# A pooled-attention and two-expert-stage kernel: the shared row tile's scores from one unpadded q, in a newly searched order

## The chip, the cores and the metric

The kernel runs on one core of one Trainium2 chip, as one program of 8,648 instructions in the profiled execution. The metric is the device time of one execution in microseconds, the median of several. TensorE (PE) multiplies matrices, VectorE (DVE), ScalarE (ACT) and GpSimd (POOL) work element by element, and SyncE (SP) issues all DMAs in order of one list.

## The reference, cut to what matters

Three stages follow each other. The change lies in the first.

```python
# 1. attention over keys and values that are averaged in groups of 8: B = 8, H = 8, S = 576, D = 64, Sp = 72
k_p = k.reshape(B, H, Sp, 8, D).mean(axis=3);  v_p = v.reshape(B, H, Sp, 8, D).mean(axis=3)
scores = np.matmul(q, k_p.transpose(0, 1, 3, 2)) / np.sqrt(D)
scores = scores - np.max(scores, axis=-1, keepdims=True)
attn = np.exp(scores); attn = attn / (np.sum(attn, axis=-1, keepdims=True) + 1e-09)
x = np.matmul(attn, v_p)                       # -> 4608 rows of 512
# 2. soft mixture of experts: 32 slots, softmax over rows into slots, w1, relu, w2, softmax over slots back
logits = x @ phi
# 3. x @ w_in (512 x 1024), h * softmax(h), layer norm, @ w_out (1024 x 512)
```

Inputs are float32: q, k and v 9.4 MB each, w1 and w2 16.8 MB each, w_in and w_out 2.1 MB each (handed over as 64-bit words that the kernel turns into float32, so 4.2 MB each are read). The output is 9.4 MB.

## The kernel before, in words

**Tiling.** The 4608 rows are 36 row tiles of 128 tokens. Three row tiles are a block (n = 0 to 11), and three blocks hold the 1152 tokens of two neighbouring batches b = 2p and 2p + 1. A batch has 576 tokens, that is four and a half row tiles, so the middle tile of the middle block (n = 1, 4, 7, 10; r = 1) holds 64 tokens of each of two batches: the shared row tile. Heads are taken in four pairs hp. `key_sums` and `key_matrix` lay the 72 pooled keys of both heads of a pair out as a matrix BD of 128 x 144 with zeros between the heads.

**The scores.** `scores(n, hp)` makes one 128 x 144 result in PSUM for each of the three row tiles: the stationary operand is q (64 + 64 rows of two heads, 128 tokens), the moving one BD. For the shared tile the kernel before keeps q in two copies of 128 columns, the first with zeros where the second batch's tokens are and the other the other way round. `load_q` loads its halves in two DMAs (L144, L145), `query_zero` writes the zeros (L371, on POOL), and two full products add up in PSUM (L386). In the trace every float32 matmul has two records, so a pair of heads of a plain block has 6 and one of blocks 1, 4, 7, 10 has 8.

**After the scores**, DVE takes row maxima (M, L394) and differences (A, L398), ACT exponentials (E), DVE their sums (U), POOL and DVE the inverse (R, r), POOL the products with it (N, L435). PE turns the result (T, L441), ACT copies it out, PE multiplies by what the values and phi give (P, X, w, x) to logits (L, L457), and weighted sums of the rows go into pG (G, L544). POOL sums the values (V), PE lays them out by key (Y, L337).

**What sets the order.** All engines run in a hand-kept order: a string of step names (`order = ...`), in which the letters above are followed by the block or batch and the piece. Each engine takes its instructions in the order of that string. The loads of q, k, v and of eight weight pieces are steps too (`ik4`, `iq7`, `ia2.0`, `ib0.0`, `io0`), so the string also is SP's order. Loads go into a ring of 88 KB in each partition in a fixed sequence of tiles, and a load waits until the tiles that it writes over have been read. SP waits with it, and all loads behind. Every load also uses one of eight DMA semaphores in turn, so it waits for the load eight places ahead to have landed. D0 to D6 are loads into the buffers of the attention stage when these come free.

**Behind the attention** stands a second string (`steps = ...`): the products with w1 (A) and w2 (B0 to B15, one for each half of an expert, L1005), the conversion of w_out and w_in (a, b, s, t, + ; `o`, `i`, `j`), the turned combine weights (p0 to p8, `combine_turn`, L976), column sums of w_out (c0 to c7, `out_sums`, L1011 and L1012). The third stage then runs over the 36 row tiles.

Of the kernel before, what the change touches and what calls it, by code (L numbers as in the profile page):

```python
# [19 lines left out]
P = 128  # L20
NP = 4
NB = 3
NR = 3
# [62 lines left out]
def moe_attention_kernel(ctx: ExitStack, tc, q, k, v, phi, w1, w2, w_in, w_out, g, out):  # L86
# [48 lines left out]
    def q_tile(n):  # L135

        nr = NR + (n % NB == 1)
        qT[n] = ring.tile([P, HP, nr, P], F32, name=f"qT{n}")

    def load_q(n, h0=0, h1=HP):  # L140
        if n % NB == 1:
            dst = qT[n].rearrange("p h r t -> p h (r t)")[:, h0:h1]
            src = q[n].rearrange("p (h x) -> p h x", h=HP)[:, h0:h1]
            sp.dma_start(dst[:, :, 0:192], src[:, :, 0:192])  # L144
            sp.dma_start(dst[:, :, 320:512], src[:, :, 192:384])  # L145
        else:
            sp.dma_start(qT[n][:, h0:h1], q[n].rearrange("p (h r t) -> p h r t", h=HP, r=NR)[:, h0:h1])
# [108 lines left out]
    if True:  # L256
# [113 lines left out]
        def query_zero(n):  # L370
            pool.memset(qT[n].rearrange("p h r t -> p h (r t)")[:, :, 192:320], 0.0)  # L371

# [7 lines left out]
        def scores(n, hp):  # L380
            sc = st["sc", n, hp] = psA.tile([P, NR, 2, J], F32, tag="sc", bufs=PT["sc"][1], name=f"sc{n}{hp}")
            x = 0
            for r in range(NR):
                hv = halves(n, r)
                for i, (b, _, _) in enumerate(hv):
                    pe.matmul(sc[:, r].rearrange("p h j -> p (h j)"), qT[n][:, hp, x, :], BD[b % NBD][:, hp, :],  # L386
                              start=(i == 0), stop=(i == len(hv) - 1))
                    x += 1
# [354 lines left out]
        for n in range(NBLK):  # L743
            if n % NB == 1:
                step(f"B{n}", query_zero, n)
# [44 lines left out]
        for x, f in zip("D0 D1 D2 D3 D4 D5 D6".split(), (scores_done, sums_done, third_group, third_slots, logits_done, fourth_group,  # L790
# [4 lines left out]
        order = ("K0.0 K0.1 k0.0 k0.1 S0.0 S0.1 K0.2 K0.3 M0.0 M0.1 A0.0 k0.3 k0.2 E0.0 E0.1 S0.2 S0.3 F0 F1 F2 F3 F4 F5 F6 F7 M0.2 U0.0 A0.2 M0.3 "  # L795
# [26 lines left out]
                 "D1 D5 e0 e1 e2 la2 lt0 es lt1 lT0 lT1 ld0 ld1 lT2 ls0 ls1 lz lo0 cs lo1 ge4").split()  # L822
        assert sorted(order) == sorted(steps)
        for x in order:
            f, args = steps[x]
            f(*args)

# [684 lines left out]
```

## Time and profile before

| what | value |
|---|---|
| three runs | 410.56, 411.17, 414.97 us; median 411.17 |
| the profiled execution | 410.22 us, span 408.4 us, mean granted clock 0.992 |
| busy share of the span | PE 94%, DVE 76%, ACT 71%, POOL 54% |
| moved by DMA | 97.09 MB; read from HBM 70.32 MB, written 9.44 MB |
| chain that ended last, by engine | PE 70%, DMA 11%, DVE 8%, POOL 4%, ACT 3% |

The span is the time from the first to the last instruction, and 1.8 us lie around it. The page cuts the span into 40 slices of 10.2 us. The attention stage is slices 1 to 12, the weights keep arriving until slice 18, and from slice 20 on the third stage repeats itself. PE's busy share is the sum of its records and is near full nearly everywhere, so the chain of waits and the stretch-by-stretch table tell more than it does. Loads are counted in MB as the trace does: a k or v of one batch is 1.18 MB, a q of one block 0.79, a piece of w1 0.52 or 1.05, one of w2 or a raw piece 1.05.

### The profile page before, as it was taken

The numbers are of one execution on the slowest core, as the hardware profiler recorded it, in microseconds if no ns is written. First come the engines' busy times: TensorE is split into PE (matmuls) and PEld (weight loads), VectorE is DVE, ScalarE is ACT, GpSimd is POOL, SyncE is SP. The second block draws the span as 40 slices with busy tenths as digits, with TensorE's granted clock in tenths as the row PEclk, the third lists the DMA queues.
The fourth block names the chain that finished last, engine by engine and source line by source line (L and its number), as shares of the span: only waits on it lengthen the run. The fifth ranks groups of instructions, "written<-read, shape, count | busy, mean of one in ns | idle before, by whom it ended". The sixth has DMA issues, their size and how long they took to land.

```text
span 408.4 us, 8648 instructions
## 1 busy us (share of the span) xinstructions
PE 383.1 (94%) x3242; PEld 231.5 (57%) x3242; DVE 310.7 (76%) x492; ACT 288.2 (71%) x600; POOL 219.9 (54%) x408
## 2 busy tenths in 40 slices
PE   3889999999999698798999999999999999999996
PEld 2868988999987153333455444444444444444445
DVE  3899979999746757965899867877777777877720
ACT  2589988988876457935699847777666776667721
POOL 4289997879630120000345776776676666766620
PEclk9999999999999899899999999999999999999999
DMA  8999999899999999990001767776667566575761
GB/s 266 391 401 377 379 315 378 314 418 413 404 373 386 416 420 411 412 412 37 0 1 28 176 121 173 175 156 128 165 95 170 147 123 165 93 172 144 124 180 51
DMA packets 86217, 97.09 MB, mean 238 GB/s; under 512 B 69920, under 2 KB 74784, under 8 KB 80416
## 3 DMA queue, kind: packets, MB, share of 16 engines
q1 hardware_dynamic: 86176, 96.55, 73.9%
q8 instruction: 25, 0.41, 0.4%
q14 instruction: 16, 0.13, 0.1%
HBM read 70.32 MB, written 9.44 MB: 195 GB/s over the span
## 4 chain that ended last, share of the span: by engine, by line
PE 70%; DMA 11%; DVE 8%; POOL 4%; ACT 3%; issue 2%; SPq 1%; DVEq 0%; POOLq 0%
PE o L1344 14%; PE o L1342 13%; PE o L1341 13%; PE sc L386 7%; PE pt L441 5%; PE plt L457 4%; DMA raw<-in_w_in_dram 3%; PE h L1251 3%; DMA w<-in_w_dram 3%; PE pG L544 3%; DMA early<-in_w_dram 2%; DMA kT<-in_k_dram 1%; POOL a_rows L435 1%; DVE early L312 1%; PE pc L976 1%
## 5 line engine op out<-in xcount | busy, mean ns | idle before, releaser
L1341 PE MATMUL o<-W_hi,vhi 128*128 128x512 f16 x280 | 106.2, 379 | 0.1
L1342 PE MATMUL o<-W_lo,vhi 128*128 128x512 f16 x280 | 106.2, 379 | 0.0
L1344 PE MATMUL o<-W_hi,vlo 128*128 128x512 f16 x280 | 66.9, 380 | 0.2 <-DMA vlo<-v 0.2
L1263 ACT ACTIVATE e<-h,nm 128x1024 f32<-128x1024 f32 x33 | 36.7, 1113 | 40.8 <-DVE nm L1256 40.8
L386 PE MATMUL sc<-early,qT 128*128 128x144 f32 x320 | 49.2, 304 | 8.1 <-ACT early L318 7.7
L1322 DVE TENSOR_TENSOR v<-v,v 128x1024 f16<-128x1024 f32 x32 | 39.2, 1225 | 14.9 <-ACT v L1305 14.9
L386 PEld LDWEIGHTS sc<-early,qT 128*128 128x128 f32 x320 | 43.8, 201 | 10.3 <-POOL sel L289 5.0
L1341 PEld LDWEIGHTS <-vhi 128*128 128x128 f16 x280 | 27.4, 98 | 33.7 <-issue 1.1
L1342 PEld LDWEIGHTS <-vhi 128*128 128x128 f16 x280 | 27.4, 98 | 32.3 <-issue 0.4
L1256 DVE TENSOR_REDUCE nm<-h 128x1 f32<-128x1024 f32 x33 | 40.4, 1223 | 5.8 <-PE h L1251 5.7
L1344 PEld LDWEIGHTS <-vlo 128*128 128x128 f16 x280 | 25.1, 98 | 33.7 <-issue 7.4
L1269 DVE CUSTOM_DVE_ANT_0 u<-h,e 128x1024 f32<-128x1024 f32 x33 | 40.3, 1223 | 5.2 <-ACT e L1263 5.1
L1305 ACT ACTIVATE v<-u,b,sr 128x1024 f32<-128x1024 f32 x33 | 40.8, 1235 | 3.5 <-POOL b L1293 3.5
L435 POOL TENSOR_TENSOR a_rows<-a_rows,rs 128x864 f32<-128x864 f32 x24 | 39.2, 1633 | 6.4 <-DVE ssum L421 2.6
L1280 ACT ACTIVATE e<-u,nmu 128x1024 f32<-128x1024 f32 x33 | 37.9, 1148 | 0.5 <-POOL nmu L1275 0.3
L1318 DVE TENSOR_SCALAR v<-u,nmu,sr 128x1024 f16<-128x1024 f32 x32 | 26.0, 812 | 11.1 <-POOL sr L1291 11.1
L447 ACT ACTIVATE late<-pt 128x384 f32<-128x384 f32 x60 | 27.7, 488 | 5.8 <-PE pt L441 4.1
L1287 POOL TENSOR_TENSOR y<-y 128x1 f32<-128x1 f32 x33 | 30.2, 915 | 2.7
L1291 POOL TENSOR_TENSOR sr<-z,exponents 128x3 f32<-128x3 f32 x33 | 29.3, 887 | 2.7
L1275 POOL TENSOR_SCALAR nmu<-st 128x1 f32<-128x1 f32 x33 | 8.5, 258 | 40.2 <-DVE st L1269 40.2
L394 DVE TENSOR_REDUCE nmax<-sc 128x6 f32<-128x432 f32 x48 | 27.5, 590 | 3.0 <-PE sc L386 2.8
L441 PE MATMUL pt<-ident,a_rows 128*128 128x128 f32 x180 | 27.6, 280 | 1.5 <-POOL a_rows L435 1.1
(253 smaller groups left out, 741.4 us busy)
## 6 DMA issues: line engine op xcount, KB each, us to landing
w<-in_w_dram SPq DMA_DIRECT2D x16, 1024.0 KB, 11.8
vT<-in_v_dram SPq DMA_DIRECT2D x8, 1152.0 KB, 11.3
out_dram<-ob SPq DMA_DIRECT2D x11, 768.0 KB, 3.6
kT<-in_k_dram SPq DMA_DIRECT2D x7, 1152.0 KB, 9.7
w<-in_w_dram SPq DMA_DIRECT2D x12, 512.0 KB, 9.6
qT<-in_q_dram SPq DMA_DIRECT2D x7, 768.0 KB, 12.4
a_rows<-in_w_dram SPq DMA_DIRECT2D x4, 1024.0 KB, 8.6
qT<-in_q_dram SPq DMA_DIRECT2D x8, 384.0 KB, 11.5
```

The source lines that it names most:

```text
L386: pe.matmul(sc[:, r].rearrange("p h j -> p (h j)"), qT[n][:, hp, x, :], BD[b % NBD][:, hp, :], start=(i == 0), stop=(i == len(hv) - 1))
L435: eng.tensor_tensor(av, av, st["rs", n, hf].unsqueeze(3).to_broadcast([P, NR, 4, J]), ALU.mult)
L441: pe.transpose(pt[:, r, :], a_buf[n % NA][:, r, CH[c]:CH[c] + P], ident)
L1256: dve.tensor_reduce(nm, ft[i][0], axis=AX.X, op=ALU.max, negate=True)
L1263: act.activation(e, hv, AF.Exp, bias=nm, accum_out=st[:, 0:1])
L1269: dve.tensor_tensor_reduce(u, hv, e, 1.0, 0.0, ALU.mult, ALU.add, st[:, 1:2])
L1280: act.activation(e, u, AF.Square, bias=nmu, accum_out=st[:, 2:3])
L1305: act.activation(v, u, AF.Identity, bias=b, scale=sr[:, 0:1])
L1322: dve.tensor_tensor(v2, u_t[i]["v"], u_t[i]["v1"], ALU.subtract)
L1341: pe.matmul(po, hi[:, c, :], W_hi[:, c, :], start=(c == 0), stop=False)
L1342: pe.matmul(po, hi[:, c, :], W_lo[:, c, :], start=False, stop=False)
L1344: pe.matmul(po, lo[:, c, :], W_hi[:, c, :], start=False, stop=(c == NFC - 1))
```

## The change

`q_tile` and `load_q` make and load every block's q alike: three row tiles without padding, 6 KB in a partition in place of 8 for blocks 1, 4, 7, 10, in one DMA. `query_zero` and its four steps B1, B4, B7, B10 are gone. For the shared row tile `scores` issues two products of 64 stationary columns, each against its own batch's BD, into partitions 0 to 63 and 64 to 127 of the same result, with `tile_position` at column 0 and 64. The number of matmuls is the same. The string `order` is another one over its whole length (the same steps without the B's), and with it the order of all five engines up to the end of the attention stage, DMAs included; because the tiles are smaller, all loads lie at other places in the ring. In the second string three things stand elsewhere: c2 ahead of B12, c4 and c5 ahead of B13, and p8 behind B13 in place of behind B14, c6 and c7.

```diff
     def q_tile(n):
-
-        nr = NR + (n % NB == 1)
-        qT[n] = ring.tile([P, HP, nr, P], F32, name=f"qT{n}")
+        qT[n] = ring.tile([P, HP, NR, P], F32, name=f"qT{n}")
 
     def load_q(n, h0=0, h1=HP):
-        if n % NB == 1:
-            dst = qT[n].rearrange("p h r t -> p h (r t)")[:, h0:h1]
-            src = q[n].rearrange("p (h x) -> p h x", h=HP)[:, h0:h1]
-            sp.dma_start(dst[:, :, 0:192], src[:, :, 0:192])
-            sp.dma_start(dst[:, :, 320:512], src[:, :, 192:384])
-        else:
-            sp.dma_start(qT[n][:, h0:h1], q[n].rearrange("p (h r t) -> p h r t", h=HP, r=NR)[:, h0:h1])
+        sp.dma_start(qT[n][:, h0:h1], q[n].rearrange("p (h r t) -> p h r t", h=HP, r=NR)[:, h0:h1])
...
-        def query_zero(n):
-            pool.memset(qT[n].rearrange("p h r t -> p h (r t)")[:, :, 192:320], 0.0)
...
-            x = 0
             for r in range(NR):
-                hv = halves(n, r)
-                for i, (b, _, _) in enumerate(hv):
-                    pe.matmul(sc[:, r].rearrange("p h j -> p (h j)"), qT[n][:, hp, x, :], BD[b % NBD][:, hp, :],
-                              start=(i == 0), stop=(i == len(hv) - 1))
-                    x += 1
+                for b, t0, t1 in halves(n, r):
+                    pe.matmul(sc[t0:t1, r].rearrange("p h j -> p (h j)"), qT[n][:, hp, r, t0:t1], BD[b % NBD][:, hp, :],
+                              start=True, stop=True, tile_position=(0, t0))
...
-            if n % NB == 1:
-                step(f"B{n}", query_zero, n)
...
```

How the engines' orders read at three places follows; names are those of the built program, a row is an instruction with its output, its inputs and the output's shape.

PE, the last two pairs of heads of block 4 (pv is a turned set of values, sc the scores' result, qT q's tile, early holds BD, pt and a_rows belong to a turned result of an earlier block). Before:

```order
L337 MATMUL pv_585<-ident,early 72x128 x4
L441 MATMUL pt_590<-ident,a_rows_160 128x128 x3
L441 MATMUL pt_594<-ident,a_rows_160 128x128 x3
L386 MATMUL sc_598<-early,qT_114 128x144 x4
L386 MATMUL sc_603<-early,qT_114 128x144 x4
```

And of the change:

```order
L329 MATMUL pv_579<-ident,early 72x128 x4
L427 MATMUL pt_584<-ident,a_rows_159 128x128 x3
L427 MATMUL pt_588<-ident,a_rows_159 128x128 x3
L373 MATMUL sc_592<-early,qT_113 128x144
L373 MATMUL sc_592<-early,qT_113 64x144 x2
L373 MATMUL sc_592<-early,qT_113 128x144
L373 MATMUL sc_597<-early,qT_113 128x144
L373 MATMUL sc_597<-early,qT_113 64x144 x2
L373 MATMUL sc_597<-early,qT_113 128x144
```

Two of the four full products of each pair have become two of 64 rows; both stand between the same neighbours, pt ahead of them.

PE, the end of the products with w2, where the last pieces of w2 are waited for (p is their result, w_70 and w_74 the halves of the last expert, pcs the column sums, of which one row of each run is shown, pc the last turned weights, p8). Before:

```order
L1005 MATMUL p_2210<-w_64_2241,hTm 32x512 x4
...
L1011 MATMUL pcs<-W_hi,ones_h 128x512
...
L1005 MATMUL p_2210<-w_70_2243,hTm 32x512 x4
...
L1011 MATMUL pcs<-W_hi,ones_h 128x512
...
L976 MATMUL pc<-ident,L_all 32x128 x16
L1005 MATMUL p_2210<-w_74_2245,hTm 32x512 x4
```

And of the change:

```order
L989 MATMUL p_2202<-w_64_2233,hTm 32x512 x4
L960 MATMUL pc<-ident,L_all 32x128 x16
L989 MATMUL p_2202<-w_70_2235,hTm 32x512 x4
...
L995 MATMUL pcs<-W_hi,ones_h 128x512
...
L989 MATMUL p_2202<-w_74_2237,hTm 32x512 x4
```

pc has moved from behind w_70's products, right ahead of w_74's, to ahead of w_70's; the two column sums ahead of w_70 went further forward.

SP, the weight loads up to the first one of w2_00, which waits for the ring (w1_60 is a piece of w1 for expert 6, raw a piece of w_out). Before:

```order
L190 DMA w1_60_142<-in_w1_dram 128x1024
L190 DMA w1_10_133<-in_w1_dram 128x1024
L190 DMA w1_20_137<-in_w1_dram 128x1024
L190 DMA w1_62_143<-in_w1_dram 128x1024
L212 DMA raw_2042<-in_w_out_dram 128x2048
L190 DMA w2_00_146<-in_w2_dram 128x2048
```

And of the change:

```order
L182 DMA w1_62_142<-in_w1_dram 128x1024
L182 DMA w2_10_147<-in_w2_dram 128x2048
L182 DMA w1_12_133<-in_w1_dram 128x1024
L182 DMA w1_10_132<-in_w1_dram 128x1024
L182 DMA w2_00_145<-in_w2_dram 128x2048
```

The load of w2_00 waits in both for the value sums V6.2 (POOL L331 before, L323 now), before also for the scores S10.3. Ahead of it now stand two pieces of w1 fewer (w1_14 and w1_60 stand behind it), so that 36.7 MB of loads are ahead of it in SP's list and not 37.8.

## Rows read from the trace of the kernel before

**Rows 1.** the page's 40 slices: PE busy tenths, GB/s by DMA

```profile
...
PE   3889999999999698798999999999999999999996
...
GB/s 266 391 401 377 379 315 378 314 418 413 404 373 386 416 420 411 412 412 37 0 1 28 176 121 173 175 156 128 165 95 170 147 123 165 93 172 144 124 180 51
...
```

**Rows 2.** Stretches: length, busy PE PEld DVE ACT POOL, PEclk, DMA share, GB/s

```profile
...
16.00:36.00 20.00, 17.50 (x160) 15.62 (x162) 19.23 (x32) 15.92 (x55) 15.14 (x13) 1.00 1.03 399
36.00:60.00 24.00, 23.22 (x318) 20.56 (x314) 22.05 (x49) 22.78 (x81) 22.17 (x22) 1.00 0.95 344
60.00:80.00 20.00, 19.82 (x301) 18.07 (x292) 19.42 (x40) 16.92 (x56) 15.53 (x19) 1.00 0.94 344
80.00:108.00 28.00, 27.91 (x437) 26.09 (x428) 25.90 (x59) 23.77 (x60) 24.20 (x24) 1.00 1.02 415
108.00:128.00 20.00, 19.82 (x385) 16.59 (x384) 10.02 (x40) 14.12 (x39) 4.84 (x5) 1.00 0.99 372
128.00:184.00 56.00, 47.42 (x582) 21.22 (x585) 40.23 (x57) 34.18 (x54) 4.07 (x6) 0.94 1.01 414
...
```

**Rows 3.** DMA rows of the stretch 24 to 28 us

```profile
...
DMA packets 255, 1.67 MB, mean 419 GB/s; under 512 B 31, under 2 KB 31, under 8 KB 158
...
```

**Rows 4.** DMA rows of the stretch 28 to 32 us

```profile
...
DMA packets 1120, 1.42 MB, mean 356 GB/s; under 512 B 46, under 2 KB 1037, under 8 KB 1072
...
```

**Rows 5.** the chain of waits from 42 to 49 us: start us, us, what

```profile
...
42.02 0.44 PE pv L337 x4
...
43.15 1.96 PE sc L386 x16
...
46.58 0.25 PE pw L348 x11
46.83 1.67 PE sc L386 x12
...
```

**Rows 6.** the chain of waits from 84 to 93 us

```profile
...
85.96 1.86 PE pG L544 x56
...
```

**Rows 7.** POOL's instructions up to 130 us: busy us, mean ns, idle before

```profile
...
L371 POOL MEMSET qT<- 128x512 f32 x4 | 2.1, 520 | 0.1
...
```

**Rows 8.** the chain of waits of the whole program, by its longer pieces

```profile
...
124.80 1.95 PE pG L544 x56
...
```

**Rows 9.** the chain of waits from 136 to 200 us

```profile
...
168.56 13.20 DMA w<-in_w_dram
181.81 1.07 PE p L1005 x8
...
183.84 1.01 PE pc L976 x32
184.85 0.90 PE p L1005 x8
...
186.06 0.67 ACT cv_y L910
...
```

**Rows 10.** PE in order of time, 174 to 200 us; in brackets idle before

```profile
...
179.31 1.07 PE L1005 MATMUL p<-w,hTm 128*32 128x512 f32 x8 [0.35 <-DMA w<-in_w_dram]
...
181.81 1.07 PE L1005 MATMUL p<-w,hTm 128*32 128x512 f32 x8 [0.46 <-DMA w<-in_w_dram]
...
```

**Rows 11.** SP in order of time, 0 to 200 us

```profile
...
99.01 10.80 SPq L190 DMA_DIRECT2D w<-in_w_dram  x6
113.40 3.62 SPq L219 DMA_DIRECT2D a_rows<-in_w_dram  x3
...
126.80 0.33 SPq L219 DMA_DIRECT2D a_rows<-in_w_dram  x1
...
```

**Rows 12.** DMA issues from 166 to 177 us: KB each, median us to landing

```profile
...
w<-in_w_dram SPq DMA_DIRECT2D x4, 1024.0 KB, 12.8
...
raw<-in_w_in_dram SPq DMA_DIRECT2D x2, 512.0 KB, 9.4
```

More of the change, by code (lines that the diff above doesn't have):

```diff
@@ L794, in moe_attention_kernel @@
         mctx.enter_context(tc.manual_schedule(engines={ET.PE, ET.DVE, ET.Activation, ET.Pool, ET.SP}))
-        order = ("K0.0 K0.1 k0.0 k0.1 S0.0 S0.1 K0.2 K0.3 M0.0 M0.1 A0.0 k0.3 k0.2 E0.0 E0.1 S0.2 S0.3 F0 F1 F2 F3 F4 F5 F6 F7 M0.2 U0.0 A0.2 M0.3 "
[26 rows of a table removed]
-                 "D1 D5 e0 e1 e2 la2 lt0 es lt1 lT0 lT1 ld0 ld1 lT2 ls0 ls1 lz lo0 cs lo1 ge4").split()
+        order = ("K0.0 K0.1 k0.0 k0.1 F0 F1 F2 F3 F4 F5 F6 F7 F8 F9 F10 S0.0 S0.1 M0.0 M0.1 A0.0 K0.2 K0.3 K1.1 K1.0 k0.3 E0.0 k0.2 E0.1 k1.1 k1.0 "
[26 rows of a table added]
+                 "e0 e1 e2 la2 lt0 es lt1 lT0 lT1 ld0 ld1 lT2 ls0 ls1 lz lo0 cs lo1 ge4").split()
         assert sorted(order) == sorted(steps)
```

56 rows, old and new, of tables (order, steps) are left out of this document.

## The prediction, on record before the changed kernel was run

> **What bounds the kernel now.** I read the page's slices first. Two things are to be seen in them: PE's digits are 9 nearly everywhere, and the DMA engines move 400 GB/s or more in the best slices up to the eighteenth, then nothing for three slices, then the steady traffic of the third stage [rows 1]. So there are two limits, and the question is which one holds where. The table by stretch answers it. From 128 to 184 us the DMA engines move 414 GB/s without a break, with a share of 1.01; I take 414 as their full rate here [rows 2]. No load can end earlier there unless more has been moved before. Before 128 us they fall short: 344 GB/s from 36 to 80 us and 372 from 108 to 128 [rows 2]. Against 414 that is 44 x 70/414 = 7.4 us and 20 x 42/414 = 2.0 us, together 9.4 us of transfer time lost. In these stretches a load waits at the head of SP's list for the ring, that is for compute: SP gets to the first load of the attention buffers only at 113.40 and to the last ones at 126.80 [rows 11]. So the attention stage's compute sets when loads go out, and these set when the weights are complete at 184 us.
>
> In the attention stage PE is busy 27.91 of 28 us from 80 to 108 us, and DVE 25.90; from 36 to 60 and from 60 to 80 us DVE has 22.05 of 24 and 19.42 of 20 [rows 2]. PE is the limit and DVE is close behind: its idle time from 36 to 108 us is 1.95 + 0.58 + 2.10 = 4.6 us. From 16 to 36 us it is DVE that is full (19.23 of 20) while PE has 17.50 [rows 2].
>
> The last piece of the path is in the chain of waits: a transfer of w2 lands at 181.76, then come its products, the column sums up to 183.84, 32 records of turned weights for 1.01 us, the products of the last half of w2 at 184.85, and ACT's work on the last words of w_in at 186.06 [rows 9]. From there to the end every engine's order is the same as before, and I count nothing.
>
> **The shared tile's products.** Two pairs of a block with a shared tile are 16 records in 1.96 us, 122 ns each, so one pair is 0.98 us [rows 5]. Two of its four products stay whole: 4 x 122 = 0.49 us. The other four records are now 64 stationary columns wide. No such pair of products side by side is in this stage, so I bound them. If they do not overlap, the nearest row is the 72-column product, 4 records in 0.44 us, 110 ns each [rows 5]: 4 x 110 = 0.44, a saving of 0.05 a pair. If they overlap as the quarter-wide products of pG do (56 records in 1.86 us, 33 ns each with four side by side, 133 ns a round, with the same 144 moving columns [rows 6]), two side by side take 66 ns each: 0.27 us, a saving of 0.22. As a far upper bound the 64-wide products could start as densely as pG's, 33 ns: 0.13, a saving of 0.36. I take 0.22, since pG's products differ from these in the width alone. With 16 pairs that is 3.5 us, with 0.8 and 5.8 as ends. The four pairs of block 1 lie where DVE is full, so they are covered; the twelve of blocks 4, 7 and 10 lie where PE is the limit: 12 x 0.22 = 2.6 us.
>
> A price stands against it. Each pair now goes from whole products to half-wide ones and back. Behind the narrow products of pw, the 12 whole records of the next block take 1.67 us, 139 ns each, against 122 behind other whole products [rows 5]: 12 x 17 ns = 0.2 us, if all of that is the change of width. Sixteen times this is 3.2 us, the upper bound of the price; the lower is nothing. I take nothing, because the slower spacing is spread over all twelve records and not put ahead of the first. [...]
>
> **The new order.** The sum of the work is the same on DVE and ACT, and POOL loses four memsets of 520 ns [rows 7], 2.1 us. They are covered by POOL's idle time from 80 us on (24.20 of 28 [rows 2]); in the two earlier stretches, where POOL is full and the value sums release ring places, they can be worth up to 1.0 us. I count nothing, since DVE is as full there. What a newly searched string gains beyond that can't be read from a profile. It can't bring more than DVE has left, 4.6 us, and it can lose. I take for the end of the attention stage 2.3 us earlier: half of DVE's idle time, a little less than what PE saves. Ends: nothing, and 4.6.
>
> **The loads.** The split q of four blocks was 4096 packets of 768 B (128 partitions, four pairs, two halves of 192 words each). Where one of them passes, 1.42 MB are moved in 4 us at 356 GB/s with 1037 packets below 2 KB; just before, 1.67 MB at 419 with 31 [rows 3, 4]. That is 0.6 us lost for one q. Three lie in the attention stage behind block 1's, so up to 1.8 us of transfer time comes free, and SP issues four loads fewer. It is worth something only where the engines have loads to move, so I use it as cover: 2.3 us earlier need 2.3 of the 9.4 us lost, and this alone gives most of it. SP's list has one place that is worse: ahead of w2_00's wait now stand 36.7 MB, no longer 37.8. It is a rival below. Then everything from 128 to 184 us moves with the attention stage: 2.3 us.
>
> **The tail.** The turned weights now stand ahead of w_70's products, in a gap in which PE waits for w2 (0.46 us before w_70's products, 0.35 before w_64's [rows 10]); the two column sums that filled it have gone further forward, so the gap is about 1.4 us (0.46 and two sums of 0.5) and takes them. Off the path go 1.01 us [rows 9]. What is late next is the last half of w2, which must land by 183.8, and the last words of w_in. The w2 loads there take a median of 12.8 us, the two raw halves 9.4 from about 177, which lets ACT start at 185 [rows 12]. I take 0.9; ends 0 and 1.0.
>
> **Sum:** 2.3 + 0.9 = 3.2 us. The profiled execution took 410.22 us: 407.0. The runs' median, 411.17, is 0.95 above it and their lowest 0.34 above, so as a median of such runs I say **407.5 us**, with 405.8 to 409.2 as this case's own range.
>
> **Rivals.**
> 1. All of PE's saving and the order come through: attention ends 4.6 us earlier, the tail gives 1.0. For it: PE is the limit in the rows, and 9.4 us of transfer time are there to be had. Against it: DVE would have to run without a break for 72 us. 410.2 - 5.6 + 0.5 = 405.1. Chance 0.20.
> 2. Only the tail arrives, 410.2 - 0.9 + 0.5 = 409.8: DVE holds the stage where it is, or the two half-wide products do not overlap, or the change of width costs its upper bound of 3.2 us and takes the 2.6 back. For it: DVE is at 93% from 80 to 108 us; the 139 ns behind pw. Against it: narrow products elsewhere in the stage do overlap fourfold. [...]
> 3. Slower: the DMA queue runs dry ahead of w2_00. SP gets to these loads at 99.01 before [rows 11], when nearly all loads ahead of it have been moved. With 1.05 MB less ahead of it, the engines stand still for 1.05/0.414 = 2.5 us unless V6.2, which releases it, comes as much earlier; it decides from the point where POOL's sums of v6 end later than 96.5. A second such dry stretch in the early gates, where the rate already is 344, would cost as much. One dry stretch with the attention stage unmoved: 410.2 + 2.5 - 0.9 + 0.5 = 412.3; with two, 414.8. For it: the reordered list, and that a stall of DMA is never made good before 184 us. Against it: the ring holds more q now, and v2 and block 4's q now stand ahead of k3, the first load that waits for the ring, so that 11.0 MB and no longer 9.0 go out before it. Chance 0.12.
>
> **How the numbers follow.** My forecast has 0.45. The range reaches over it, the larger part of rival 1 and rival 2, and leaves out the slow half of rival 3 and the fast end of rival 1: 404.5 to 411.6. One per cent, about what a measurement of this kernel can tell from no change, is 4.1 us, so faster means below 407.1: nearly all of rival 1 and four tenths of my own case, 0.19 + 0.18 = 0.37. Slower, above 415.3, needs rival 3 with two stretches or something that I do not see: 0.07. The rest, 0.56, is within.
>
> **What would show it.** In the profile after, the pairs of blocks 4, 7 and 10 should take about 0.76 us for 8 records and not 0.98. The last pG products of the attention stage should start near 122.5 us, not 124.80 [rows 8], and the last load of its buffers near 124.5. The rate from 36 to 80 us should be above 350 GB/s, and no packets of 768 B should be left. Ahead of the last p products there should be no pc on the chain, and ACT's words of w_in should start about 3 us earlier than 186.06. The third stage should keep its 200 us. I am wrong if the pairs still take 0.9 us or more, if the attention stage ends earlier and 184 does not move (then DMA was the limit all along), or if a stretch between 85 and 110 us shows less than 400 GB/s.

## The result: slower by 1.0%, and the profile after

The changed kernel takes **415.47 us** (median of 20 runs, 412.16 to 417.50); the kernel before, beside it, 410.88 us (20 runs, 408.84 to 415.09). The ratio is **1.0104, interval 1.0078 to 1.0129**. I had said 407.5 us, range 404.5 to 411.6. The profiled execution took 413.71 us with a span of 411.4, 3.0 us more than before. Ratios here and below leave out the executions in the slow state, three of 775 to 989 us among them. The medians differ by 4.6 us, the spans of the two profiled executions by 3.0: the traces below explain the 3.0, and no trace shows the other 1.6.

The page's slices of the changed kernel, PE's busy tenths and the rate of the DMA engines, answer to [rows 1]:

```profile
PE   6779999989989799787999999999999999999996
GB/s 279 409 416 416 417 403 395 186 397 278 382 312 379 374 420 419 418 417 155 0 1 22 156 133 178 179 126 143 167 99 159 145 133 158 103 164 144 129 178 51
```

Up to the seventh slice the transfers are now nearly full, and then comes a hole (186 in the eighth) and more of them up to the twelfth. By stretch, columns as in [rows 2], with three stretches of 4 us added:

```profile
36.00:60.00 24.00, 22.82 (x287) 19.04 (x281) 22.86 (x49) 21.62 (x78) 20.06 (x19) 1.00 1.00 410
60.00:80.00 20.00, 20.00 (x264) 17.45 (x265) 18.14 (x38) 17.19 (x59) 14.22 (x18) 1.00 0.77 306
80.00:108.00 28.00, 26.14 (x402) 23.15 (x397) 24.14 (x53) 21.71 (x54) 21.15 (x22) 1.00 0.90 343
108.00:128.00 20.00, 18.24 (x367) 15.76 (x364) 9.52 (x37) 14.69 (x39) 7.00 (x6) 1.00 0.93 347
128.00:184.00 56.00, 48.73 (x673) 23.18 (x671) 42.29 (x69) 36.69 (x61) 4.17 (x6) 0.97 1.00 404
76.00:80.00 4.00, 4.00 (x46) 3.63 (x47) 3.63 (x11) 3.48 (x9) 2.09 (x4) 1.00 0.06 8
92.00:96.00 4.00, 4.00 (x36) 3.47 (x35) 2.92 (x7) 2.81 (x9) 2.47 (x2) 1.00 0.59 191
120.00:124.00 4.00, 4.00 (x82) 3.76 (x81) 1.07 (x5) 3.21 (x9) 0.00 (x0) 1.00 0.63 223
```

Two things are to be seen. The transfers gain 24 x 66 = 1.6 MB from 36 to 60 us and lose 0.8, 2.0 and 0.5 MB in the next three stretches. And PE, which had 27.91 of 28 us from 80 to 108 [rows 2], has 26.14, and 18.24 of 20 behind that: 3.4 us are missing. The chain of waits says where. First pairs of heads of shared tiles, one and then two [rows 5], then the gaps and the last gather, the weighted sums that go into pG [rows 6, 8], then the tail [rows 9]:

```profile
40.69 1.11 PE sc L373 x8
42.90 2.17 PE sc L373 x16
...
89.39 1.86 issue
...
117.09 1.76 issue
...
129.43 1.95 PE pG L530 x56
...
172.58 15.11 DMA w<-in_w_dram
...
187.73 1.11 PE p L989 x8
...
189.14 0.66 ACT cv_y L894
```

A pair takes 1.09 us, not 0.76 as I forecast and not 0.98 as before. Twice PE stands for 1.8 us with "issue", which means that it waits for nothing that the profile shows. The last gather starts at 129.43 and not 124.80 [rows 8], the words of w_in at 189.14 and not 186.06 [rows 9]: 4.6 us late, of which 3.1 are left at the end. SP's timeline has the holes' cause, answering to [rows 11]:

```profile
63.27 0.43 SPq L204 DMA_DIRECT2D raw<-in_w_out_dram  x1
78.78 0.33 SPq L182 DMA_DIRECT2D w<-in_w_dram  x1
...
116.44 5.48 SPq L211 DMA_DIRECT2D a_rows<-in_w_dram  x3
```

From 63.7 to 78.78 us SP issues nothing: the load at its head (`ia1.3`) needs the ring place of block 8's q, and that block's last scores are made up to 78.7. The attention buffers' first loads go out at 116.44, not 113.40.

The first gap in PE's timeline (the bracket is the idle time ahead of a row):

```profile
87.82 0.73 PE L530 MATMUL pG<-a_rows,dmix 128*32 128x145 f32 x16
88.31 1.08 PE L530 MATMUL pG<-a_rows,d 128*32 128x145 f32 x25
91.24 0.45 PE L530 MATMUL pG<-a_rows,d 128*32 128x144 f32 x7 [1.86 <-issue]
```

It falls in the middle of a gather whose products all have their inputs. In the queues' table of 88.8 to 89.9 us stands one packet of an instruction queue:

```profile
q8 instruction: 1, 0.02, 5.3%
```

It is 16 KB and was moved from 88.87 to 89.81; PE went on at 91.24. At the second gap such a packet passed from 116.49 to 117.56, and PE went on at 118.85. The trace has 26 such packets of 16 KB (25 in the span, one behind it) and 6,600 records of PE, its sequencer's among them: 254 a packet. That these packets bring PE's instructions, a block in each, is my reading of these numbers; no row says it. So my theory after the result was: **PE ran out of instructions**, because a block of them came late. (The expectations below call the blocks pages.)

### The profile page after: what moved, and what is told of

It reads as the page before. It is cut to its first block, busy times and chain, and to the rows that moved or that the text cites. A ratio compares the mean times of both kernels' runs of the same rounds, so it can differ in the third digit from the quotient of the medians.

```text
span 411.4 us, 8643 instructions
## 1 busy us (share of the span) xinstructions
PE 383.5 (93%) x3242; PEld 226.8 (55%) x3242; DVE 311.1 (76%) x492; ACT 287.6 (70%) x600; POOL 218.0 (53%) x404
## 4 chain that ended last, share of the span: by engine, by line
PE 70%; DMA 14%; ACT 5%; DVE 4%; POOL 3%; issue 3%; SPq 1%; DVEq 0%; ACTq 0%
PE o L1328 14%; PE o L1326 13%; PE o L1325 13%; PE sc L373 7%; PE pt L427 5%; DMA w<-in_w_dram 4%; PE h L1235 3%; DMA late<-in_w_dram 3%; PE plt L443 3%; DMA vT<-in_v_dram 3%; PE pG L530 3%; DMA W_lo<-in_w_out_dram 3%; ACT a_rows L393 1%; PE p L821 1%; DMA kT<-in_k_dram 1%
## 5 line engine op out<-in xcount | busy, mean ns | idle before, releaser
L1247 ACT ACTIVATE e<-h,nm 128x1024 f32<-128x1024 f32 x33 | 36.7, 1113 | 40.8 <-DVE nm L1240 40.8
L373 PE MATMUL sc<-early,qT 128*128 128x144 f32 (+1 forms) x320 | 48.6, 309 | 6.4 <-ACT early L310 5.0
L373 PEld LDWEIGHTS sc<-early,qT 128*128 128x128 f32 (+1 forms) x320 | 38.4, 184 | 13.8 <-ACT early L310 5.4
L1338 ACT ACTIVATE ob<-o,r 128x512 f32<-128x512 f32 x32 | 21.7, 678 | 9.5 <-PE o L1328 9.5
```

The lines of the kernel that those rows point to most:

```text
L373: pe.matmul(sc[t0:t1, r].rearrange("p h j -> p (h j)"), qT[n][:, hp, r, t0:t1], BD[b % NBD][:, hp, :], start=True, stop=True, tile_positio ...
L1247: act.activation(e, hv, AF.Exp, bias=nm, accum_out=st[:, 0:1])
```

## The experiments

Ratios are against runs of the kernel before on the same chip. First each part alone.

**The products alone**, in the old order and with the padded q:

```diff
-                    pe.matmul(sc[:, r]..., qT[n][:, hp, x, :], BD[b % NBD][:, hp, :], start=(i == 0), stop=(i == len(hv) - 1))
+                    pe.matmul(sc[t0:t1, r]..., qT[n][:, hp, x, t0:t1], BD[b % NBD][:, hp, :], start=True, stop=True, tile_position=(0, t0))
```

> The kernel before with one edit: the shared tile's four products of a pair of heads are two whole ones and two of 64 stationary columns, taken from the padded q as it was; order, loads and ring stay. Theory (width): going from whole products to 64-wide ones and back costs PE more than the side-by-side pair saves. Then a pair of blocks 1, 4, 7, 10 takes about 1.09 us, as in the changed kernel, not 0.98; twelve pairs on PE's path make 12 x 0.11 = 1.3 us, so about 411.5 us as a profiled execution, 1.003 of the kernel before. Rival (place): the pairs are slow in the changed kernel because of what stands around them in its order; then they take 0.76 to 0.98 us here and the time is 0 to 2.6 us below the kernel before.

Measured: 411.40 us, ratio 0.9991 (0.9957 to 1.0024). The chain of this kernel has two pairs, and three:

```profile
38.34 2.17 PE sc L385 x16
...
67.13 3.25 PE sc L385 x24
```

1.085 us a pair, so it is the width and not the place. The starts of one pair's eight records (the next pair starts at 68.050) show how:

```
whole 66.964  67.089 | 64 wide 67.305 67.312  67.478 67.485 | whole 67.701  67.927
```

The two products side by side start 7 ns apart, so they overlap. But the step into them takes 216 ns in place of the 122 to 125 of a whole record, the next round 173, the step out 223 and the record behind that 226. Against 122 each that is 0.35 us for going to half width and back, more than the 0.25 us that the overlap saves. The time hardly moves: 12 x 0.11 = 1.3 us are 0.3%, at the edge of the interval. In the profile they don't reach the end of the stage either: the last gather starts at 124.48, before at 124.80, and from block 3's last scores to it are 89.6 us in both (one execution each). So in the old order other waits seem to have taken the 1.3 us up.

**The tail alone**, the second string:

```diff
-  c0 c1 B12 c2 c3 +i1 bi2 si2 G6 g7 B13 c4 c5 ti2 B14 c6 c7 p8 B15
+  c0 c1 c2 B12 c3 c4 c5 +i1 bi2 si2 G6 g7 B13 p8 ti2 B14 c6 c7 B15
```

> The kernel before with the second string of the changed kernel alone: c2 ahead of B12, c4 and c5 ahead of B13, the last turned weights (p8) behind B13. Theory: the 32 records of p8 leave the path behind the last half of w2, so the third stage starts 0.9 to 1.2 us earlier than 190.68 us and the time is about 409.2, 0.997 of the kernel before. Rival: PE has no gap there, since the column sums that filled it are gone only in part; then no change within 0.3 us.

Measured: 411.03 us, 0.9987 (0.9945 to 1.0028). The interval holds the theory's 0.997 and the rival's 1.000; the profile is clearer, and it shows the rival. SP's last two loads of w_in, the last p products, and the first of w_in's words on ACT:

```profile
177.83 1.43 SPq L212 DMA_DIRECT2D raw<-in_w_in_dram  x2
...
185.76 1.06 PE L1005 MATMUL p<-w,hTm 128*32 128x512 f32 x8 [0.47 <-DMA w<-in_w_dram]
187.17 0.66 ACT L910 ACTIVATE cv_y<-raw 128x512 f32<-128x512 f32 x1
```

The turned weights are off the path, and PE waits for w2 instead. ACT starts 9.3 us behind the issue of w_in's last loads, before 9.5 (176.54 to 186.06), in the changed kernel 8.9 (180.26 to 189.14). So the transfers set it: in the trace of before the two loads take 9.0 and 9.9 us to landing. This execution too had a gap, of 1.99 us with "issue" at 88.97, although PE's order and the loads up to there are those of the kernel before, whose profile has at that place 0.09 us. So such a gap can differ between executions of the same instructions.

**The first string alone**, with padded q and the steps that write zeros right ahead of each shared block:

> The kernel before with the first string of the changed kernel alone (the four steps that write zeros stand right ahead of the first pair of their block); q stays padded, the products whole, the second string old. Theory (order): the new order makes the load queue wait too long in the third quarter of the attention stage and moves page borders of PE's instructions; then the last products of the attention stage start 2 to 5 us after 124.80, and the time is 1 to 5 us above the kernel before. Rival (products): the order alone is worth the 2.3 us that I forecast, and only the pairs and the smaller ring places spoil it; then the last ones start near 122.5 and the time is about 408. In either case the pairs take 0.98 us.

Measured: 429.91 us, 1.0397 (1.0326 to 1.0468). Inconclusive: PE waited 4.5 us for a write of zeros at the place I gave it, 5.1 for DVE at another. The string fits tiles of its own sizes only, and what it is worth by itself is not told by this.

Next the loads. **Four loads moved** in the changed kernel:

```diff
-  ia1.3 iv7 ir4 io1 ir7 ia2.2     ...  ia6.1 ib1.0 ia1.1 ia1.0 ib0.0
+  io1 ir7 ia1.3 iv7 ir4 ia2.2     ...  ia1.1 ia1.0 ia6.1 ib1.0 ib0.0
```

> The changed kernel with four loads at other places in SP's list: the raw piece io1 and ir7, which wait for nothing in the ring, ahead of ia1.3, which waits for the last scores of block 8; ia1.1 and ia1.0 ahead of ia6.1, which waits for the last scores of block 9. Theory (dry queue): 1.8 MB more stand ahead of the wait, so the DMA engines no longer stand still from 76 to 80 us, and there is no stretch below 300 GB/s from 92 to 100; about 2.5 to 4 us of transfer come back. If transfers set the end, 184 us comes back and the time is 410 to 412 us. Rival (compute): the attention stage's own end, 129.4 us for the last pG products, sets the last loads, and it stays where it is; then the stretch from 76 to 80 fills, the engines stand still as long later on, and the time stays within 0.7 us of the changed kernel's 413.7.

Measured: 413.97 us, 1.0064 (1.0025 to 1.0102). 76 to 80 us are filled (361 GB/s), but 92 to 96 has 202 and 104 to 108 now 223. What I had not expected is on PE: no gap is left, and the last gather starts at 125.78.

**The changed kernel again, and two variants of it**, on one chip. In the second, the row tiles of some shared pairs are taken in another order, so that the narrow products of two pairs touch:

```diff
-            for r in range(NR):
+            for r in TURN.get((n, hp), range(NR)):      # (0, 2, 1) in one pair, (1, 0, 2) in the next
```

In the third all weight loads stand in the order in which their ring places come free: `io1 ir7 ia1.3 iv7 ia1.2 ia1.1 ia1.0 ir4 ia2.2 ia2.3 ib1.0 ia6.1 ia6.0 ib0.0 ia6.3 ia6.2 ib0.1 ib1.1`. The fourth is the old order and padded q with narrow products, turned pairs and the new tail.

> The changed kernel once more, unchanged, beside the kernel before and the next two kernels on the same chip. Theory (fetch by execution): the two gaps of 1.8 us in which PE waits for nothing that the trace shows belong to that one execution, in which PE's instruction pages came late, since the same PE order in the run with moved loads showed none. Then they are gone or stand elsewhere here, and the last pG products start near 125.8 us without them and 1.8 us later for each. Rival (fetch by order): the order puts page borders ahead of dense runs of small products; then both gaps stand again in the first and the second pG and the last products start near 129.4. Time: about 1.010 of the kernel before.

> The changed kernel with the three row tiles of eight of the sixteen shared pairs in another order, 0 2 1 in one pair and 1 0 2 in the next, so that the 64-wide products of two pairs stand next to each other four times; all else stays. Theory (switch): in the records the two 64-wide products of a pair start 7 ns apart, so they do overlap; the records around each change of width come 50 to 104 ns later than the usual 122, about 0.35 us a pair. Then two neighbouring pairs take about 1.82 us in place of 2.17, and the time falls by 4 x 0.35 = 1.4 us at most, 0.3%, which five rounds can hardly tell. Rival (width): it is the 64-wide products themselves that are slow; then two pairs keep 2.1 to 2.2 us.

> The changed kernel with the weight loads behind vT6 in the order in which their ring places come free in the trace (io1, ir7, ia1.3, iv7, the rest of ia1, ir4, ia2.2, ia2.3, ib1.0, ia6.1, ia6.0, ib0.0, ia6.3, ia6.2, ib0.1, ib1.1). Theory (dry queue): nothing that is free stands behind a wait; 76 to 80 and 92 to 100 us are filled, and the end of the w2 loads comes 1.5 to 3 us earlier than in the changed kernel, so the time is 411 to 413, 1.000 to 1.004 of the kernel before. Rival (compute): the buffers of the attention stage come free no earlier, all ring loads have landed by then in either case, so a stretch dries up later, from 104 to 114 us, and the time stays within 0.2% of the run with the first four loads moved, 1.006.

> The kernel before with its old first string, padded q, the 64-wide products in the turned order (six times two pairs next to each other) and the new second string: what the runs so far point to as the best of both. Theory (switch): the twelve pairs next to each other take 0.91 us each, below the 0.98 before, the other four 1.09, and the tail gives 1 us; together 0.4 + 1 = 1.4 us below the kernel before, 0.997. Rival: the edits are lost in the stage's other waits (DVE and the ring); then no change within 0.3%.

Measured: again 416.58 us, 1.0143 (1.0108 to 1.0178); turned 414.66, 1.0120 (1.0084 to 1.0156); **loads sorted 411.54, 1.0022 (0.9991 to 1.0054)**; old order turned 411.88, 1.0027 (0.9998 to 1.0057). So the order of 18 loads is worth 1.2%, 5 us. My theory that the gaps belonged to one execution fell for the new order: both stand at the same two places in the first two, here of the unchanged kernel,

```profile
90.61 0.45 PE L530 MATMUL pG<-a_rows,d 128*32 128x144 f32 x7 [1.86 <-issue]
117.96 0.28 PE L530 MATMUL pG<-a_rows,d 128*32 128x145 f32 x1 [1.50 <-issue]
```

and neither in the one with sorted loads, whose last gather starts at 125.37 and not 130.18. Yet its transfers are not better at the end. They stand still later, as the rival said:

```profile
104.00:108.00 4.00, 4.00 (x66) 3.60 (x67) 3.13 (x10) 2.87 (x8) 2.26 (x5) 1.00 0.41 132
112.00:116.00 4.00, 4.00 (x84) 3.37 (x79) 1.93 (x6) 3.27 (x9) 1.68 (x2) 1.00 0.38 82
```

The turned pairs behave as the switch theory says. Two neighbours in the old order:

```profile
38.34 1.82 PE sc L387 x16
```

0.91 us a pair where the narrow products touch, 1.09 where they don't. In the new order the chain's three pairs from 65 us on take 3.10 us with one such meeting, 3.45 without. The time shows nothing of it (1.0027 and 1.0120).

**Where the blocks end.** I counted PE's records, as above, up to each gap. In twelve gaps of seven executions (two each in five of the changed kernel's family, one in the run of the tail, one in that of the padded order) the last record ahead of the gap has number 1984 or 1985, or 2752 or 2753. These are 768 apart, which is three blocks of 256 if a whole number of blocks of about 254 records lies between them. 256 is my estimate from these two numbers, here and in the next expectation; no row shows a block's end. When the packet starts, PE has 5 to 37 records left up to that place in the twelve; in the 18 passes of the same two places without such a gap, in ten executions, it has 110 to 184. So I moved the ends that this estimate gives and left the loads as they were:

```diff
+            if (n, hp) == (0, 1):
+                for i in range(52):
+                    x = 32 * (i % 4)
+                    pe.matmul(st["busy"][x:x + 32, 0:32], ident[:, x:x + 32], ident[:, x:x + 32], start=True, stop=True, tile_position=(0, x))
```

> The changed kernel, loads and order as they are, with 52 small products of 32 x 32 (their result is not used) behind the second pair of block 0, where PE waits 4.1 us for the key matrix. They shift the borders of PE's 256-instruction pages by 208 instructions. Theory (pages): in all seven gaps seen so far PE stops right behind its instruction 193 modulo 256 and goes on 1.3 to 1.5 us after a 16 KB packet of the instruction queue; with the borders elsewhere, away from the dense pG products, no gap above 1.3 us is left in pG, the last pG products start near 126 us in place of 129 to 130, and the time falls by about 3 us, to 1.003 to 1.007 of the kernel before, although the stretches without loads stay (76 to 80, 92 to 96 us). Rival (loads): the gaps are only a sign of the badly ordered loads and stay wherever PE is dense, or they go and the end of the loads stays near 190; then the time stays at 1.010 to 1.014.

Measured: **412.85 us, 1.0034 (1.0000 to 1.0067)**, with 208 more instructions and the loads of the changed kernel. No gap is left in any gather. The last one, though, starts at 128.96, not 126, because this execution lost 4 us at its start: a load of v landed at 18.73 and not 16.98, and then the granted clock fell:

```profile
16.00:36.00 20.00, 16.30 (x115) 13.30 (x114) 15.49 (x30) 12.06 (x43) 14.24 (x14) 0.83 0.95 370
...
128.96 1.95 PE pG L534 x56
```

From the end of block 2's scores (33.1 us here, 28.8 in the changed kernel, 29.1 with sorted loads) to the last gather it is 95.9 us, against 100.6 in the changed kernel, 3.6 of them gaps, and 96.3 with sorted loads. So with the loads as they were and no gaps, the stage is as short as with sorted loads (one execution each), and the time falls from 1.010 and 1.014 to 1.003. The late start hides most of it in this execution, which took 413.47 us, against 413.71 of the changed kernel's; its mean clock, 0.979, is that of all twelve (0.978), so the others probably lost time there too. The dry stretches cost, beside the gaps, little that these runs can measure.

**Why a block would come late.** If a block waited behind the loads that were issued ahead of it, the two halves of the first load experiment would part:

> The changed kernel with io1 and ir7 alone moved ahead of ia1.3. Theory (backlog): the page packets of PE wait behind the data loads issued before them; with these 1.8 MB moved before the wait, fewer loads are issued in one burst from 79 to 83 us, ahead of the page that PE needs at 89, so the first gap (1.8 us, near 89) goes; the second, near 116, depends on later loads and stays, or goes with the shift of 1.8 us. The last pG products start near 127.5 us in place of 129 to 130. Rival (chance): both gaps stay or the pages' lateness shows no relation to the loads moved.

> The changed kernel with ia1.1 and ia1.0 alone moved ahead of ia6.1, which waits for block 9's scores. Theory (backlog): 1.0 MB more is issued in the burst from 79 to 84 us; the first late page comes no earlier than 2.5 us behind its border or later still, so the first gap stays at 1.8 us or grows; the stretch from 92 to 96 us is filled better than in the changed kernel. Rival (chance): the first gap goes here too, although more is queued ahead of the page.

Measured: `io1 ir7` alone moved 413.00 us, 1.0048 (1.0008 to 1.0089); `ia1.1 ia1.0` alone 415.62, 1.0115 (1.0028 to 1.0201). Both profiles have both gaps, the first one 1.77 and 1.80 us. The first kernel's profile is one of its four slower executions (414.5 to 416.3 us; the other six took 411.9 to 413.3), so the six may have lacked a gap: no trace shows it. That profile has transfers from 76 to 80 us and a hole behind the gap:

```profile
76.00:80.00 4.00, 4.00 (x37) 3.63 (x39) 3.63 (x11) 3.48 (x8) 2.52 (x4) 1.00 0.92 383
92.00:96.00 4.00, 4.00 (x36) 3.46 (x34) 2.54 (x7) 2.71 (x8) 2.40 (x3) 1.00 0.21 59
```

Nearly all queued loads had been moved when its packet started at 89.16, and I took that as the end of my backlog theory. It is not: a packet that waited behind loads would start just when they have been moved. The traces say more if one counts from where PE passes the record 256 ahead of each place, by the estimate the end of the block before (1729 for the first, 2497 for the second), to the start of the packet. At the first place that is 4.2 to 5.2 us in the seven executions with a gap and 2.5 to 3.5 in the eight without; at the second 5.7 to 6.0 in five and 2.7 to 4.2 in ten. With `io1 ir7` alone, 1.6 MB of loads were moved in that time, from 84.95 to 89.16. In three runs with sorted loads nothing was moved behind the end near 114 us, and the packet started after 0.5 us.

So a wait behind data fits, but it is not shown. The amount queued doesn't tell the delay: with all four loads moved, five loads were under way at record 1729, here three, and the packet came after 2.6 us. And behind the first gap here the next packet started 2.1 us after PE went on, while almost nothing was moved. What is shown is that the order of the loads matters: in the new order all five profiles with the loads as they were or half moved have both gaps, and all five with four loads moved or sorted have none. How stays open, and the run of the tail shows that the order isn't all.

**The best version.** Sorted loads with turned pairs, run twice; then the same with eight busy products (steps F, whose results are not used) moved into PE's early wait:

```diff
-  F0 F1 F2 F3 F4 F5 F6 F7 F8 F9 F10 S0.0 S0.1 M0.0
+  F0 F1 F2 S0.0 S0.1 F3 F4 F5 F6 F7 F8 F9 F10 M0.0
```

> The changed kernel with the loads in the order of their ring places (as in the run that did that alone) and four times two shared pairs next to each other with the 64-wide products together. Theory (sum): no gap in PE, no dry stretch before 104 us, and 4 x 0.35 us less on PE: 1.002 less 0.003, so 0.999 of the kernel before, the best of the runs with the new order. Rival (DMA end): the buffers of the attention stage come free no earlier, so the last load lands near 187 us again and the time stays at 1.002.

> The kernel with the loads in the order of their ring places and the 64-wide products of neighbouring pairs together, once more, for a second interval: 0.998 of the kernel before if the first one was right; above 1.000 if it was luck. Again no gap above 1.3 us in pG, and the last pG products near 124.6 to 125.4 us.

> The same kernel with eight of the busy products F3 to F10 behind the second pair of block 0, in the 4.1 us in which PE waits for the key matrix. Theory (clock): in the new order PE is idle from 8.4 to 12.5 us and the granted clock is 0.50 from 12 to 16 and 0.71 from 16 to 20 us, where the kernel before has 1.00; with PE kept busy the 44 records from 12.55 on take less than their 8.13 us, block 1's scores end about 1 us earlier than 20.4, and the time falls by 0.5 to 1 us, 0.002, since DVE is nearly full behind them. Rival (DVE): DVE is busy 3.59 to 3.96 of every 4 us there and sets the pace, so nothing changes behind 24 us and the time stays that of the other kernel.

> The kernel with busy products in PE's wait of block 0, for its profile alone: granted clock 0.9 to 1.0 from 12 to 20 us in place of 0.50 and 0.71, and block 1's scores ending about 1 us earlier than 20.4 us (theory clock), or the same clock and the same time behind 24 us (rival DVE).

Measured: 410.94 us, 0.9979 (0.9950 to 1.0007), and 411.07, 1.0003 (0.9974 to 1.0032): the first was in part luck, and the kernel is level with the one before. With the busy products 410.52, 0.9986 (0.9959 to 1.0012); a profiled execution of it took 408.37 us, with no gap in the gathers and the last one at 124.51. The stretch from 12 to 16 us without and with them:

```profile
12.00:16.00 4.00, 3.45 (x14) 3.46 (x15) 3.59 (x5) 3.56 (x19) 0.28 (x1) 0.50 1.02 420
```

```profile
12.00:16.00 4.00, 2.25 (x14) 1.82 (x14) 3.41 (x4) 3.90 (x20) 0.11 (x1) 1.00 1.02 417
```

The granted clock is 1.00 in place of 0.50, but the last record of block 1's scores starts at 20.1 us, against 20.4 and 20.0 in the two profiles without them: from 16 to 20 us DVE is busy 3.86 of 4 us in both kernels, so it sets the pace there, as the rival said. So by the ratios this version is more than 1% faster than the changed kernel (1.0104), and that it is faster than the kernel before is not shown.

## Why the prediction was wrong

**What bounds the kernel** was right in the main. The end follows the attention stage, with a scatter of 3 us (us):

| kernel | last gather starts | w_in's last words on ACT | span |
|---|---|---|---|
| before | 124.80 | 186.06 | 408.4 |
| products alone | 124.48 | 185.11 | 407.4 |
| changed | 129.43 | 189.14 | 411.4 |
| four loads moved | 125.78 | 187.66 | 410.0 |
| first two of them | 131.19 | 191.25 | 413.7 |
| blocks' ends moved | 128.96 | 189.65 | 411.7 |
| best version without busy products | 124.60 | 187.00 | 409.5 |
| the same again | 125.00 | 185.42 | 408.9 |
| with busy products | 124.51 | 184.47 | 406.6 |

In sixteen profiled executions, these among them, 59.5 to 62.4 us lie from the second column to the third and 222.1 to 224.0 from there to the end. Wrong was that the 9.4 us of lost transfer time were there to be had: what can be loaded before the attention buffers come free is bounded by the ring, so transfers that run ahead early stand still later, as the dry stretches of the sorted loads show.

**The new order is the step that failed.** I took 2.3 us earlier, with nothing as the lower end, after writing that a new order can lose. It came 4.6 us later. Two gaps with "issue", in which by my theory PE lacked instructions, are 1.86 + 1.76 = 3.6 us; the shared pairs add 1.3 to PE's work (next point); together 4.9, so if the pairs' price reached the end, the rest of the new order gave back about 0.3. No row that I had read has such a gap, and none of my rivals had it. The trace of the kernel before shows how near it was. At the same place its packet passed from 87.03 to 88.08, PE went on 1.4 us behind that, and the chain of waits has

```profile
89.43 0.09 issue
```

The bound was at fault all the same: for a step whose gain "can't be read from a profile", the lower end must be a loss.

**The shared pairs.** The overlap was right: 0.76 forecast, 8 records at two side by side are 0.73 without the switch. The price of the width was not: I took nothing and 0.2 us as the upper bound, from products of another width, and it is 0.35. So a saving of 2.6 us of PE's time became a cost of 1.3. In the old order that cost didn't show at the end of the stage (the products alone), so PE's 27.91 of 28 us need not mean that every product there is on the path. The records show the 0.35 us, over four starts; what PE does in that time they don't show. Rival 2, to which the other three chances leave 0.23, had the change of width as one of its three ways, at 3.2 us; at 0.35 a pair it is 16 x 0.35 = 5.6.

**Rival 3**, the dry queue, has the time that came, but not the reason. The queue did run dry, ahead of block 8's and block 9's last scores and not where I put it. Filling the first stretch alone left both gaps; taking away the gaps alone, with the loads left as they were, gave 1.0034.

**The loads** that no longer come in 768-byte packets (4096 of them before, none now): 410 GB/s from 36 to 60 us and 415 from 16 to 36. Over 36 to 80 us it is 363, above the 350 that I asked for, and it was worth nothing, for the reason above.

**The tail** was mis-sized: 0.9 us forecast, nothing measurable came. I named what is late next, the last words of w_in, but let ACT start on them at 185: 9.4 us behind "about 177" is 186.4. By the trace of before, the first of the two loads was issued at 176.54 and took 9.0 us, so it landed at 185.5, and ACT started 0.5 us behind that. No more than this half microsecond was to be had. The third stage kept its time.

## What to carry to other kernels

In a run of small, dense products look for an idle "issue" in the middle of a group whose inputs are all there, beside a packet of an instruction queue. Here two of 1.86 and 1.76 us cost more than I had forecast the whole change to gain, 3.2, and four loads moved or 208 instructions more ahead of them made them go. Put narrow products of neighbours together: here a pair took 0.91 us where they touch and 1.09 where they don't. Time saved in an early transfer counted here only if the memory to load into was free: with sorted loads the rate from 60 to 80 us was 398 GB/s and no longer 306, but then 132 from 104 to 108 and 82 from 112 to 116.

## What the runs showed of the hardware

- **Gaps beside instruction packets.** All twelve gaps of 1.5 to 2.0 us lie at two places in PE's records that are 768 apart, and none was left in the run with 208 instructions put in ahead. That late blocks of instructions are the cause is my theory, their 256 records my estimate (254 a packet, 768 = 3 x 256). The packet starts 0.4 to 0.9 us ahead of the gap and takes 0.9 to 1.1 us; PE goes on 1.3 to 1.5 us behind the packet. In one execution two such gaps are 3.6 us.
- **Half width and back** costs 0.35 us between float32 products of 144 columns, in the old order and the new: 1.09 us a pair alone, 0.91 if two pairs share it.
- **The clock.** In the best version without busy products PE is idle from 8.4 to 12.5 us and the granted clock is 0.50 from 12 to 16 and 0.71 from 16 to 20; with eight products in that wait it is 1.00 in both stretches. Over all runs the mean clock is 0.985 in the changed kernel, 0.990 before and 0.988 with these products.
